# A tail search with fewer steps, and second experts' codes written to memory

## The chip, the cores and the metric

The kernel runs on one core of a Trainium2 chip. The metric is the device time of one execution in microseconds (us). The core's engines work side by side, each on its own queue in order: TensorE (PE, matrix products into PSUM), VectorE (DVE), ScalarE (ACT), GpSimd (POOL) and SyncE (SP, which issues most transfers). GpSimd issues the indirect transfers, those that gather or scatter rows by a list of indices.

## The reference

```python
attn = np.maximum(z @ z.T / S, 0) ** 2           # 4 batches, S = 3072, d_qk = 64
x = (u * (attn @ v)).reshape(12288, 256)
# first mixture: 8 experts of 1536 tokens each, tokens taken in falling order of logits
for idx in np.argsort(-(x @ w_gate).flatten()):
    tok, e = divmod(idx, 8)
    if assigned[tok] >= 0 or counts[e] >= 1536: continue
    assigned[tok] = e; counts[e] += 1
y[assigned == e] = relu(x[assigned == e] @ w1[e]) @ w2[e]
# second mixture: argmax expert, the first 384 tokens of each expert in order are kept
out[i] = gate[i] * (relu(y[i] @ w1b[e2]) @ w2b[e2]) if kept else 0
```

Since the second mixture keeps the first 384 tokens of each expert, the kernel runs the first mixture for the first 40 x 128 tokens alone and verifies at the end (`check`) that these were enough; a raised flag runs `general` over all tokens.

## The kernel before

There are four stages. **Attention** fills TensorE for the first 1106 us; each fp32 product is made of three with operands split into a high and a low part. Most of the routing is done beside it: a threshold splits the tokens into a head, whose experts are settled, and a tail, whose rows are scattered to a table `tt`.

**First mixture** (`ffn1`). Sixteen units in an order written out by hand: units 0 to 7 take 432 head tokens of each expert (4 tiles of at most 128 rows, table `TA`), units 8 to 15 take 256 tokens of each expert (2 tiles, table `TB`), which head and tail tokens fill up. A unit has 8 steps f = 0 to 7, each with 6 products of layer 1 (`L1013`) and, two steps behind, 6 of layer 2 (`L1163`). ScalarE makes `hH` and VectorE `hL` of each layer 1 result; weights are split by ScalarE (`pH`) and VectorE (`pL`, `L225`), four pieces a unit. Around the products hooks do the rest: rows of unit n+2 are gathered at f = 6 (`fetch`, on GpSimd), the next unit's rows are turned by TensorE, and the finished unit's rows with the second gate's logits (`yr`) are scattered to `ya` (`post`). `code` then finds each row's second expert: `first_hot` gives a number `M` per row. `hot` and `rh` (VectorE, one pair a tile) are one-hot rows of the token's place, and `mapping` multiplies them on TensorE into `pe2` (`L1150`), a table of 128 x 40 second experts that `table2` reads when the last unit is done. `slow` is a list of such VectorE work, taken one by one at fixed places (`trickle`).

**The tail search** (`tail`) runs beside units 0 to 7. It assigns 23 columns of tail tokens in 9 phases. In a phase, each token's best open expert `V`, `TH` is found; the threshold at which some expert runs full is found by three rounds of a grid of 32 values: VectorE compares (`gG`, `L856` for the first round and `L858` for the others), TensorE counts with 23 products (`L866`), the count is compared with the room left (`gO`, `L868`), a product spreads it (`L871`) and `gX` sums it. Then `NW` marks the chosen tokens, a product counts them (`L890`), and full experts are closed. After the phases a closing part gives each token a slot, builds the table `tabB` by 23 one-hot products (`L587`), and `tokens` turns it into index lists for units 8 to 15.

`tail` is a generator. Each `yield` names planner costs, and `Follow.step`, called after nearly every product of `ffn1`, issues the next step when it seems due: `tp` is TensorE's planned time (a product of w columns adds w/2400), `td` VectorE's. A step (pe, d, extra, lead) does this:

```python
m.tp += pe
m.dve(d, 0.2)                      # td = max(td, tp + 0.2) + d
self.ready = m.td + 0.15 - lead    # the next step waits until tp >= ready
m.td += extra
```

The fetch of unit 8 needs the lists, so in unit 7 at f = 3 `late` calls `p.finish()`, which issues all the steps that are left at once.

**Closing and second mixture.** `table2` ranks the second experts and builds lists by one-hot products; `ffn2` runs 8 units of 384 rows and scatters `orow` to the output.

Of the kernel before, what the change touches and what calls it, by code (L numbers as in the profile page):

```python
# [53 lines left out]
class Follow:  # L54
# [24 lines left out]
class Moe:  # L79
# [55 lines left out]
    def consts(self, wg1, wg2):  # L135
# [3 lines left out]
        self.idr = c.tile([128, 128], FR, name="idr")  # L139
        nc.scalar.activation(self.idr, self.idf, AF.Copy)  # L140
# [67 lines left out]
    def zero_tail(self):  # L208
        self.nc.sync.dma_start(self.tt.rearrange("(p c) k -> p (c k)", c=self.TC), self.zt[:, :self.TC * self.TW])
# [379 lines left out]
    def tokens(self, tj, tp, H, name, rows):  # L589
# [11 lines left out]
        nc.vector.scalar_tensor_tensor(s, f, -1.0, e, op0=OP.add, op1=OP.add)  # L601
        return dict(tj=tj, tp=tp, g=g, s=s)
# [78 lines left out]
    def prep(self):  # L681
# [71 lines left out]
        self.TA = self.tokens(self.tabH[:, 0], self.tabH[:, 1], 6 * E, "a", JF * 128)  # L753
# [30 lines left out]
    def tail(self, rows):  # L784
# [26 lines left out]
        nc.vector.tensor_scalar(iv, tok[:, :TD], 0.5, -1e36, op0=OP.is_lt, op1=OP.mult)  # L811
# [12 lines left out]
        nc.vector.scalar_tensor_tensor(LT[:, TD:], H[:, :, None].to_broadcast([128, 4, E]), -1e36,  # L824
# [3 lines left out]
        self.diag(k8, kcol)  # L828
        nc.vector.tensor_scalar(cl0, k8, 0.5, 0.0, op0=OP.is_lt, op1=OP.add, accum_out=cc)
        hi = self.t0  # L830
        PH = E + 1
        cl, c2, NW = cl0, cc, None
        for ph in range(PH):
            LM = R.tile(sh, F32, name="LM")
            nc.vector.scalar_tensor_tensor(LM, cl[:, None, :].to_broadcast(sh), -1e30, LT, op0=OP.mult, op1=OP.add)
            s3 = R.tile([128, 3], F32, name="s3")
            if ph:

                nc.vector.scalar_tensor_tensor(s3, sd[:, 0], d, sd[:, 1], op0=OP.mult, op1=OP.add)
                cc = c2  # L840
                yield 0.0, 0.5, 0.0, 0.5
            else:
                nc.vector.tensor_scalar(s3, w3, st, None, op0=OP.mult)
            V = R.tile([128, TC], F32, name="tV")
            nc.vector.tensor_reduce(V, LM, AX.X, OP.max)
            M = R.tile([128, NTH], F32, name="gM")
            nc.vector.tensor_scalar(M, self.mrow, s3[:, 0:1], hi, op0=OP.mult, op1=OP.add)
            TH = R.tile(sh, BF, name="tTH")
            nc.vector.tensor_tensor(TH, LM, V[:, :, None].to_broadcast(sh), OP.is_equal)
            yield 0.0, 0.85 if ph else 2.0, 0.0, 0.5  # L850
            for i in range(3):
                G = R.tile([128, TC, NTH], BF, name="gG", tag="gG", bufs=1)
                Vb = V[:, :, None].to_broadcast([128, TC, NTH])
                Mb = M[:, None, :].to_broadcast([128, TC, NTH])
                if i == 0:
                    nc.vector.tensor_tensor(G, Vb, Mb, OP.is_ge)  # L856
                else:
                    nc.vector.scalar_tensor_tensor(G, Vb, sn, Mb, op0=OP.subtract, op1=OP.is_ge)  # L858
                    hi = self.plus(hi, sn)
                if i < 2:  # L860
                    M = R.tile([128, NTH], F32, name="gM")
                    nc.vector.tensor_scalar(M, self.mrow, s3[:, i + 1:i + 2], hi, op0=OP.mult, op1=OP.add)
                yield 0.25, 1.2 if i else 0.9, 0.3
                pc = self.rt()
                for j in range(TC):
                    nc.tensor.matmul(pc[:E, :NTH], TH[:, j, :], G[:, j, :], start=j == 0, stop=j == TC - 1)  # L866
                over = R.tile([E, NTH], BF, name="gO")
                nc.vector.tensor_scalar(over, pc[:E, :NTH], kcol, None, op0=OP.is_gt)  # L868
                yield 0.6, 0.2
                pa = self.rt()  # L870
                nc.tensor.matmul(pa[:, :NTH], self.ones[:E, :], over, start=True, stop=True)  # L871
                x = R.tile([128, NTH], F32, name="gX")
                sn = R.tile([128, 1], F32, name="gn")
                nc.vector.scalar_tensor_tensor(x, pa[:, :NTH], 0.5, s3[:, i:i + 1].to_broadcast([128, NTH]),
                                               op0=OP.is_lt, op1=OP.mult, accum_out=sn)
            hi = self.plus(hi, sn)
            NW = R.tile(sh, BF, name="tNW")
            nc.vector.scalar_tensor_tensor(NW, V[:, :, None].to_broadcast(sh), hi, TH, op0=OP.is_ge, op1=OP.mult)
            nc.vector.scalar_tensor_tensor(LT, NW, 1e35, LT, op0=OP.mult, op1=OP.add)
            if ph < PH - 1:  # L880
                dd = R.tile([128, 3], F32, name="std")
                sd = R.tile([128, 2, 3], F32, name="stw")
                nc.vector.tensor_scalar(dd[:, 1:2], s3[:, 2:3], 1.0 / NTH, None, op0=OP.mult)
                nc.vector.tensor_scalar(dd[:, 0:1], hi, self.lo0, -1.0 / NTH, op0=OP.subtract, op1=OP.mult)
                nc.vector.tensor_scalar(sd[:, 1], w3, dd[:, 1:2], None, op0=OP.mult)
                nc.vector.tensor_tensor(dd[:, 2:3], dd[:, 0:1], dd[:, 1:2], OP.subtract)
                nc.vector.tensor_scalar(sd[:, 0], w3, dd[:, 2:3], None, op0=OP.mult)
            yield 0.25, 0.9, 1.0
            pn = self.rt()
            nc.tensor.matmul(pn[:, :TC * E], self.ones, NW.rearrange("p j g -> p (j g)"), start=True, stop=True)  # L890
            cn = R.tile([128, E], F32, name="tcn")
            nc.vector.tensor_reduce(cn, pn[:, :TC * E].rearrange("p (j g) -> p g j", g=E), AX.X, OP.add)
            if ph < PH - 1:
                cl = R.tile([128, E], F32, name="cl")
                c2 = R.tile([128, 1], F32, name="cc")
                d = R.tile([128, 1], F32, name="std2")
                nc.vector.scalar_tensor_tensor(cl, cn, 0.0, k8, op0=OP.add, op1=OP.is_ge, accum_out=c2)
                nc.vector.tensor_tensor(d, c2, cc, OP.is_gt)
                yield 0.3, 0.7, 0.0, 0.5
        self.over = c.tile([128, E], F32, name="ovr")  # L900
        nc.vector.tensor_tensor(self.over, cn, k8, OP.is_gt)
        yield 0.6
        FIN = R.tile(sh, BF, name="FIN", bufs=1)
        nc.vector.tensor_scalar(FIN, LT, 1e34, None, op0=OP.is_ge)

        NF = self.JF * 128
        m = R.tile([128, TC], F32, name="tm", bufs=1)
        nc.vector.tensor_scalar(m, tok, NF + 0.5, None, op0=OP.is_lt)
        oh = R.tile([128, E, TC], F32, name="toh", bufs=1)
        nc.vector.tensor_tensor(oh, FIN.rearrange("p j g -> p g j"), m[:, None, :].to_broadcast([128, E, TC]),  # L910
                                OP.mult)
        rs = c.tile([128, E, TC], F32, name="trs")
        nc.gpsimd.memset(rs, 1.0)
        nc.gpsimd.memset(rs[:, :, 0:1], 0.0)
        yield 0.6
        inc = R.tile([128, E, TC], F32, name="tinc", bufs=1)
        nc.vector.tensor_tensor_scan(inc.rearrange("p g j -> p (g j)"), rs.rearrange("p g j -> p (g j)"),
                                     oh.rearrange("p g j -> p (g j)"), 0.0, op0=OP.mult, op1=OP.add)
        tot = R.tile([128, E], BF, name="ttot", bufs=1)
        nc.vector.tensor_copy(tot, inc[:, :, TC - 1])  # L920
# [154 lines left out]
    def ffn1(self, units, W, keys, plan, src, dst, ncol, side0, G, X, late=()):  # L1075
# [100 lines left out]
        def hook(n, f):  # L1176
            if f == 3 and n > 1:
                mapping(n - 2)
# [328 lines left out]
def fast(ctx, tc, m, w1, w2, w1b, w2b, out, ahead, rows):  # L1507
    E = m.E
# [97 lines left out]
```

## Time and profile before

| what | value |
|---|---|
| median of three runs | 1636.5 us (1636.49 to 1637.97) |
| profiled execution | 1636.56 us |
| span of its instructions | 1634.8 us |
| TensorE busy | 1580.8 us (97%) |
| VectorE busy | 1186.5 us (73%) |
| ScalarE busy | 1116.7 us (68%) |
| GpSimd busy | 333.1 us (20%) |
| mean granted TensorE clock | 0.983 |

The profiled execution is 0.06 us from the median, so its views can stand for the runs. Products on TensorE are pipelined: a record's duration is longer than the distance to the next start, and the distance is the cost. A line number is that of the function that issues the instruction, so instructions of helpers are told apart by their tiles.

### The profile page before, as it was taken

How to read it: one execution, taken by the hardware profiler on the slowest of the kernel's cores; microseconds unless marked ns; L12 is line 12 of the kernel's file. 1: busy time of each engine (PE TensorE's matmuls, PEld its weight loads, DVE VectorE, ACT ScalarE, POOL GpSimd, SP SyncE). 2: the span in 40 equal slices, each digit the busy share in tenths (PEclk: the TensorE clock that was granted, in tenths of full speed). 3: DMA queues.
4: the chain of work that ended last, by engine and by line, in shares of the span. 5: the costliest groups of instructions: out<-in, count | busy, mean ns of one | idle time of the engine just before them, and what ended most of it. 6: DMA issues, size and time to landing. Idle time of an engine off the chain costs nothing.

```text
span 1634.8 us, 24914 instructions
## 1 busy us (share of the span) xinstructions
PE 1580.8 (97%) x8570; PEld 1326.7 (81%) x8570; DVE 1186.5 (73%) x2338; ACT 1116.7 (68%) x1937; POOL 333.1 (20%) x518
## 2 busy tenths in 40 slices
PE   8999999999999999999999999999999969989997
PEld 5888887888888888888887777878888759978997
DVE  6877788777778767777877877677777766775652
ACT  7877788777788877778987767884444316644552
POOL 1000000000000000000000478642333113323341
PEclk9999999999999999999999999999999969999999
DMA  6111355322335212224310112223343204644540
GB/s 136 20 27 33 68 136 133 73 70 76 72 67 130 76 46 59 59 66 86 77 33 21 28 20 45 60 80 118 101 124 103 84 19 134 189 134 124 153 129 28
DMA packets 282681, 132.44 MB, mean 81 GB/s; under 512 B 216717, under 2 KB 268173, under 8 KB 282544
## 3 DMA queue, kind: packets, MB, share of 16 engines
q1 hardware_dynamic: 269264, 106.90, 26.0%
q0 software_dynamic: 13280, 23.85, 5.0%
q8 instruction: 69, 1.13, 0.3%
q14 instruction: 68, 0.56, 0.1%
HBM read 84.61 MB, written 40.55 MB: 77 GB/s over the span
## 4 chain that ended last, share of the span: by engine, by line
PE 70%; issue 16%; DVE 7%; POOL 2%; ACT 2%; DMA 1%; SPq 1%; POOLq 0%; DVEq 0%
PE acc L397 12%; PE acc L398 12%; PE acc L399 12%; PE sc L1013 9%; PE sc L368 6%; PE sc L369 6%; PE acc L1163 5%; PE mi L1114 2%; DVE pL L225 1%; PE rt L866 1%; PE mi L336 1%; PE acc L1320 1%; PE acc L1321 1%; PE acc L1322 1%; DVE hL L1023 1%
## 5 line engine op out<-in xcount | busy, mean ns | idle before, releaser
L382 DVE TENSOR_TENSOR aL<-a,aH 128x512 fp32r<-128x512 f32 x576 | 398.6, 693 | 212.9 <-ACT a L377 157.8
L371 ACT ACTIVATE r<-sc 128x512 f32<-128x512 f32 x576 | 343.0, 595 | 186.6 <-PE sc L369 180.7
L397 PE MATMUL acc<-aH,pH 128*128 128x512 f32 x1152 | 449.7, 390 | 0.0
L398 PE MATMUL acc<-aL,pH 128*128 128x512 f32 x1152 | 449.0, 390 | 0.0
L399 PE MATMUL acc<-aH,pL 128*128 128x512 f32 x1152 | 448.5, 389 | 0.0
L379 DVE TENSOR_TENSOR a<-r 128x512 f32<-128x512 f32 x344 | 238.5, 693 | 43.0 <-ACT r L371 41.8
L397 PEld LDWEIGHTS acc<-aH,pH 128*128 128x128 f32 x1152 | 216.7, 188 | 45.6
L399 PEld LDWEIGHTS acc<-aH,pL 128*128 128x128 f32 x1152 | 216.7, 188 | 45.6
L398 PEld LDWEIGHTS acc<-aL,pH 128*128 128x128 f32 x1152 | 216.7, 188 | 45.5
L368 PE MATMUL sc<-zHL 128*128 128x512 f32 x576 | 229.8, 399 | 6.3 <-DVE zHL L280 6.0
L1021 ACT ACTIVATE hH<-sc 128x432 fp32r<-128x432 f32 (+2 forms) x192 | 90.0, 469 | 212.5 <-PE sc L1013 208.2
L369 PE MATMUL sc<-zLH,zHL 128*128 128x512 f32 x576 | 225.3, 391 | 0.2 <-DVE zLH L284 0.2
L380 ACT ACTIVATE aH<-r 128x512 fp32r<-128x512 f32 x344 | 217.8, 633 | 10.9
L347 POOL TENSOR_TENSOR lgs<-lgb 32x128 f32<-32x128 f32 x23 | 15.2, 659 | 853.2 <-DVE lgb L344 853.2
L376 ACT ACTIVATE aH<-r 128x512 fp32r<-128x512 f32 x232 | 146.7, 632 | 7.4
L1023 DVE SCALAR_TENSOR_TENSOR hL<-sc,hH 128x432 fp32r<-128x432 f32 (+2 forms) x192 | 99.3, 523 | 65.6 <-ACT hH L1021 65.4
L377 ACT ACTIVATE a<-r 128x512 f32<-128x512 f32 x232 | 142.8, 616 | 0.0
L368 PEld LDWEIGHTS sc<-zHL 128*128 128x128 f32 x576 | 108.7, 189 | 36.1 <-DVE zHL L280 7.4
L1013 PE MATMUL sc<-xTH,pH 128*128 128x384 f32 (+2 forms) x368 | 125.9, 342 | 5.9 <-DVE hL L1023 5.8
L369 PEld LDWEIGHTS sc<-zLH,zHL 128*128 128x128 f32 x576 | 108.8, 189 | 21.5 <-DVE zLH L284 0.5
L1013 PE MATMUL sc<-xTL,pH 128*128 128x384 f32 (+2 forms) x368 | 120.0, 326 | 0.0
L1013 PE MATMUL sc<-xTH,pL 128*128 128x384 f32 (+2 forms) x368 | 119.8, 326 | 0.0
(333 smaller groups left out, 2261.4 us busy)
## 6 DMA issues: line engine op xcount, KB each, us to landing
raw<-in_moe_w_dram SPq DMA_DIRECT2D x84, 512.0 KB, 3.7
raw<-in_v_dram SPq DMA_DIRECT2D x24, 512.0 KB, 4.3
uraw<-in_u_dram SPq DMA_DIRECT2D x192, 64.0 KB, 2.3
out_dram<-zt SPq DMA_DIRECT2D x24, 512.0 KB, 4.2
xb<-xT SPq DMA_DIRECT2D x14, 512.0 KB, 3.4
zr<-in_z_dram SPq DMA_DIRECT2D x96, 64.0 KB, 2.4
zLH<-zHL POOLq DMA_DIRECT2D x46, 128.0 KB, 2.3
ya<-zt SPq DMA_DIRECT2D x10, 544.0 KB, 3.5
```

The lines of the kernel that those rows point to most:

```text
L368: nc.tensor.matmul(p, lw, zHL[b, c % QC], start=True, stop=False)
L369: nc.tensor.matmul(p, lw, zLH[c], start=False, stop=True)
L371: nc.scalar.activation(r, p, AF.Relu, scale=SCALE)
L376: nc.scalar.activation(HS[s], r, AF.Square)
L377: nc.scalar.activation(a, r, AF.Square)
L379: nc.vector.tensor_tensor(a, r, r, OP.mult)
L380: nc.scalar.activation(HS[s], r, AF.Square)
L382: nc.vector.tensor_tensor(LS[s], a, HS[s].bitcast(F32), OP.subtract)
L397: nc.tensor.matmul(accs[h], vh[sl], HS[s], start=k == 0, stop=False)
L398: nc.tensor.matmul(accs[h], vh[sl], LS[s], start=False, stop=False)
L399: nc.tensor.matmul(accs[h], vl[sl], HS[s], start=False, stop=k == KT - 1)
L1013: nc.tensor.matmul(p, a, b[:, d, :w], start=i == 0, stop=i == 5)
```

## The change

**Search.** The grid is compared in units of the step: `U = (V - hi) / st`, so that the values compared with are constants (`m3`), and a position `N` takes the place of the moving upper end. The comparison with the room left goes from VectorE to ScalarE (a `Relu` with `-kcol` as bias), and so do `h`, `fine` and `dd`, once a phase. The yields become fewer and their numbers change; a new form of five numbers doesn't go through `td`. The constants 1e30 to 1e36 become multiples of the step (`mk`). Work that doesn't depend on the phases is moved ahead of them, the last count behind the table.

```diff
+                if len(y) == 5 if isinstance(y, tuple) else False:
+                    m.tp += y[0]
+                    self.ready = m.tp + y[4]
+                    return
...
-                yield 0.0, 0.5, 0.0, 0.5
...
-            yield 0.0, 0.85 if ph else 2.0, 0.0, 0.5
...
-                yield 0.25, 1.2 if i else 0.9, 0.3
...
-                nc.vector.tensor_scalar(over, pc[:E, :NTH], kcol, None, op0=OP.is_gt)
-                yield 0.6, 0.2
...
-            yield 0.25, 0.9, 1.0
...
-                nc.vector.tensor_tensor(d, c2, cc, OP.is_gt)
-                yield 0.3, 0.7, 0.0, 0.5
...
+            LM = R.tile(sh, F32, name="LM", bufs=1)
+            nc.vector.scalar_tensor_tensor(LM, cl[:, None, :].to_broadcast(sh), mk[:, 1:2], LT, op0=OP.mult, op1=OP.add)
+            V = R.tile([128, TC], F32, name="tV")
+            nc.vector.tensor_reduce(V, LM, AX.X, OP.max)
+            if ph:
+                d = R.tile([128, 1], F32, name="std2")
+                nc.vector.tensor_tensor(d, c2, cc, OP.is_gt)
+                st = R.tile([128, 1], F32, name="st")
+                nc.vector.scalar_tensor_tensor(st, dd, d, fine, op0=OP.mult, op1=OP.add)
+                cc = c2
+            U = R.tile([128, TC], F32, name="tU")
+            rs = R.tile([128, 1], F32, name="trs1")
+            nc.vector.reciprocal(rs, st)
+            nc.vector.tensor_scalar(U, V, hi, rs, op0=OP.subtract, op1=OP.mult)
+            for i in range(3):
...
+                if i == 0:
+                    nc.vector.tensor_tensor(G, bc(U), Mb, OP.is_le)
+                    TH = R.tile(sh, BF, name="tTH")
+                    nc.vector.tensor_tensor(TH, LM, V[:, :, None].to_broadcast(sh), OP.is_equal)
+                else:
+                    nc.vector.scalar_tensor_tensor(G, bc(U), N, Mb, op0=OP.subtract, op1=OP.is_le)
+                yield 0.25, 1.45 if i else 2.2
...
+                nc.scalar.activation(over, pc[:E, :NTH], AF.Relu, bias=kcol)
+                yield 0.8, 0.0, 0.0, 0.0, 0.45
...
+                N = self.plus(N, sn) if i else sn
...
+                nc.scalar.activation(h, N, AF.Identity, scale=st, bias=hi)
...
+                nc.scalar.activation(fine, st, AF.Copy, scale=float(NTH) ** -3)
...
+                nc.scalar.activation(dd, hi, AF.Abs, scale=1.0 / NTH, bias=lon)
+                nc.vector.scalar_tensor_tensor(dd, dd, -1.0, fine, op0=OP.mult, op1=OP.subtract)
+            nc.vector.scalar_tensor_tensor(LT, NW, mk[:, 0:1], LT, op0=OP.mult, op1=OP.add)
...
+            yield 0.25, 1.1, 0.5
```

**Closing part of the search.** The table covers only the slots that units 8 to 15 use, 2 columns per expert in place of 6, so its 23 products write 32 columns, not 96; the slots are computed in one code with fewer operations, and the yields ahead of the table go from five to two.

```diff
-        s = self.slot_code(inc, oh, TC)
-        yield 1.1
...
-        yield from self.table(px, s, TC, 6 * E, jv, pv, pool=False)
...
+        yield 0.25, 2.0
...
+        yield 0.3, 1.3
         px = self.rt("tabt")
+        yield from self.table(px, None, TC, 2 * E, jv, pv, pool=False, i=s)
```

**Codes through memory.** For units 0 to 12 (`ND` = 13) the number `M` of each row is scattered, one word a row, to a table `ea` in device memory, by index lists `c` that `tokens` makes; `hot`, `rh` and the products into `pe2` stay for the last three units. `ea` is zeroed in attention, read back in the last unit at f = 2 and added to `pe2`.

```diff
+            def put(t, h):
+                m = min(128, w - t * 128)
+                self.put_rows(ea, T["c"][:m, h:h + 1], M[0][:m, t:t + 1], ncol * 128 - 1, ecodes)
+
+            if n < ND:
+                self.slow.append((0.35, add))
+                self.slow.append((0.8, lambda: M.append(self.first_hot(lg, E, len(cols), None))))
+                self.slow.extend((0.0, lambda t=t, h=h: put(t, h)) for t, h in enumerate(cols))
+                return
...
+            if f == 2 and n == NU - 1:
+                self.pe2a = self.r1.tile([128, ncol], F32, name="pe2a%d" % ncol)
+                nc.sync.dma_start(self.pe2a, ea.rearrange("(p j) k -> p (j k)", p=128))
...
         mapping(NU - 1)
+        nc.vector.tensor_tensor(self.pe2a, self.pe2a, pe2[:, :ncol], OP.add)
```

**Buffers.** `idr`, which nothing reads, goes; the three `orow` tiles of a unit of `ffn2` become slices of one tile that shares `yT`'s buffer.

## Rows read from the trace of the kernel before

**Rows 1.** The page, part 2: 40 slices, busy tenths, granted clock in tenths.

```profile
PE   8999999999999999999999999999999969989997
...
PEclk9999999999999999999999999999999969999999
```

**Rows 2.** Windows: stretch, us, busy us by engine, PEclk, DMA share, GB/s.

```profile
1104.00:1303.40 199.40, 196.21 (x1447) 166.04 (x1445) 151.68 (x468) 83.59 (x145) 59.11 (x86) 1.00 0.35 108
1303.40:1331.80 28.40, 9.79 (x147) 7.33 (x147) 21.04 (x82) 0.00 (x0) 0.97 (x3) 0.54 0.02 6
1331.80:1338.00 6.20, 6.20 (x24) 5.71 (x22) 2.80 (x18) 0.93 (x2) 3.14 (x5) 0.62 0.14 42
1338.00:1458.50 120.50, 116.08 (x942) 112.87 (x940) 80.58 (x215) 71.34 (x147) 39.25 (x53) 1.00 0.51 154
```

**Rows 3.** Timeline of PE, 1301 to 1312.5: start us, us, instruction, idle before.

```profile
1301.27 0.37 PE L1150 MATMUL pe<-rh,hot 128*128 128x40 bf16 x4
1301.57 0.73 PE L1114 MATMUL mi<-sel,yT 128*128 128x136 f32 x4
...
1303.41 0.73 PE L866 MATMUL rt<-gG,tTH 128*8 128x32 bf16 x23
...
1308.16 0.31 PE L890 MATMUL rt<-tNW,ones 128*128 128x184 bf16 x1 [0.93 <-DVE tNW L878]
1311.80 0.78 PE L866 MATMUL rt<-gG,tTH 128*8 128x32 bf16 x23 [3.33 <-DVE gG L856]
```

**Rows 4.** Timeline of VectorE: the first grid of two search phases (six more between).

```profile
1122.42 0.92 DVE L856 TENSOR_TENSOR gG<-tV,gM 128x736 bf16<-128x736 f32 x1
...
1296.21 0.92 DVE L856 TENSOR_TENSOR gG<-tV,gM 128x736 bf16<-128x736 f32 x1
```

**Rows 5.** Groups of VectorE by form, 1104 to 1303: busy us, mean ns, idle.

```profile
L225 DVE TENSOR_TENSOR pL<-raw,pH 128x1024 fp32r<-128x1024 f32 x28 | 34.1, 1216 | 0.7 <-ACT pH L220 0.5
L858 DVE SCALAR_TENSOR_TENSOR gG<-tV,gn,gM 128x736 bf16<-128x736 f32 x15 | 14.8, 985 | 0.5
...
L1139 DVE TENSOR_SCALAR rh<-iob,tabH,fM 128x40 bf16<-128x40 bf16 x24 | 5.5, 291 | 0.0
L868 DVE TENSOR_SCALAR gO<-rt,kcol 8x32 bf16<-8x32 f32 x22 | 5.3, 239 | 21.7 <-PE rt L866 21.6
```

**Rows 6.** Waits of TensorE, 1104 to 1303: us in total, times, longest.

```profile
PE sc L1013 <- DVE hL L1023: 2.2, 4, 1.1
```

**Rows 7.** Groups of ScalarE by form, whole span.

```profile
L220 ACT ACTIVATE pH<-raw 128x1024 fp32r<-128x1024 f32 x80 | 84.1, 1051 | 0.0
...
L1021 ACT ACTIVATE hH<-sc 128x256 fp32r<-128x256 f32 x64 | 24.6, 384 | 35.1 <-PE sc L1013 34.2
...
L1345 ACT ACTIVATE orow<-acc,gt 128x256 f32<-128x256 f32 x16 | 7.6, 472 | 3.2 <-PE acc L1322 2.2
...
L1306 ACT ACTIVATE ex<-l 128x24 f32<-128x24 f32 x8 | 1.8, 223 | 8.7 <-DVE l L1304 8.6
L279 ACT ACT_TABLE_LOAD x1 | 1.3, 1283 | 0.7 <-PEq L1587 0.7
```

**Rows 8.** Timeline of GpSimd, 1180 to 1193.

```profile
1180.40 1.00 POOL L969 DMA_INDIRECT g<-xa,tkga  x1 [5.45 <-PE rt L871]
1181.70 0.97 POOL L969 DMA_INDIRECT g<-xa,tkga  x1 [0.30 <-issue]
...
1192.24 1.59 POOL L636 DMA_INDIRECT ya<-yr,tksa  x1 [6.11 <-ACT yr L1117]
```

**Rows 9.** Waits of TensorE, 1365 to 1458.

```profile
PE sc L1013 <- DVE hL L1023: 3.6, 6, 0.6
```

**Rows 10.** Timeline of VectorE, 1402 to 1403.

```profile
1402.50 0.49 DVE L1139 TENSOR_SCALAR rh<-iob,tabB,fM 128x40 bf16<-128x40 bf16 x2
1402.90 0.75 DVE L1023 SCALAR_TENSOR_TENSOR hL<-sc,hH 128x256 fp32r<-128x256 f32 x2
```

**Rows 11.** Timeline of VectorE, 1465.

```profile
1465.81 0.20 DVE L1254 TENSOR_TENSOR off<-s,off 128x40 f32<-128x40 f32 x1
```

More of the change, by code (lines that the diff above doesn't have):

```diff
@@ L587, in table, with tokens @@
                 nc.tensor.matmul(p[:, :2 * H], L[:, :, j], rf[:, :, j], start=o + j == 0, stop=o + j == ncol - 1)
-    def tokens(self, tj, tp, H, name, rows):
+    def tokens(self, tj, tp, H, name, rows, codes=False):
         nc = self.nc
@@ L601, in tokens @@
         nc.vector.scalar_tensor_tensor(s, f, -1.0, e, op0=OP.add, op1=OP.add)
+        if codes:
+            c = self.r1.tile([128, H], I32, name="tkc" + name)
+            nc.vector.scalar_tensor_tensor(q, tp, float(rows // 128), tj, op0=OP.mult, op1=OP.add)
+            nc.vector.scalar_tensor_tensor(c, q, -float(rows // 128), e, op0=OP.add, op1=OP.add)
+            return dict(tj=tj, tp=tp, g=g, s=s, c=c)
         return dict(tj=tj, tp=tp, g=g, s=s)
@@ L828, in tail @@
         self.diag(k8, kcol)
+        nc.vector.tensor_scalar(kcol, kcol, -1.0, None, op0=OP.mult)
         nc.vector.tensor_scalar(cl0, k8, 0.5, 0.0, op0=OP.is_lt, op1=OP.add, accum_out=cc)
[L830 to L840, printed above, removed]
-                yield 0.0, 0.5, 0.0, 0.5
[L842 to L849, printed above, removed]
-            yield 0.0, 0.85 if ph else 2.0, 0.0, 0.5
[L851 to L862, printed above, removed]
-                yield 0.25, 1.2 if i else 0.9, 0.3
[L864 to L867, printed above, removed]
-                nc.vector.tensor_scalar(over, pc[:E, :NTH], kcol, None, op0=OP.is_gt)
-                yield 0.6, 0.2
[L870 to L887, printed above, removed]
-            yield 0.25, 0.9, 1.0
[L889 to L897, printed above, removed]
-                nc.vector.tensor_tensor(d, c2, cc, OP.is_gt)
-                yield 0.3, 0.7, 0.0, 0.5
@@ L912, in tail @@
[L912 to L920, printed above, removed]
@@ new lines, in tail @@
+        early = R.tile([128, TC], F32, name="tm", bufs=1)
+        nc.vector.tensor_scalar(early, tok, NF + 0.5, None, op0=OP.is_lt)
+        rs1 = c.tile([128, E, TC], F32, name="trs")
+        nc.gpsimd.memset(rs1, 1.0)
+        nc.gpsimd.memset(rs1[:, :, 0:1], 0.0)
+        base = R.tile([128, E], F32, name="tbase", bufs=1)
+        nc.vector.tensor_scalar(base, self.hc, float(self.WA), 127.0 - self.WA, op0=OP.max, op1=OP.add)
+        nc.vector.scalar_tensor_tensor(base, self.iof[:, :E], 256.0, base, op0=OP.mult, op1=OP.add)
@@ L937, in tail @@
         nc.vector.tensor_scalar(pv, ti[:, 2], 1.0, None, op0=OP.add)
[L938 to L945 removed]
+        hi = self.t0
@@ new lines, in tail @@
+        oh = R.tile([128, E, TC], F32, name="toh", bufs=1)
+        nc.vector.scalar_tensor_tensor(oh, LT.rearrange("p j g -> p g j"), mk[:, 3:4],
+                                       early[:, None, :].to_broadcast([128, E, TC]), op0=OP.is_ge, op1=OP.mult)
+        inc = R.tile([128, E, TC], F32, name="tinc", bufs=1)
+        flat = lambda x: x.rearrange("p g j -> p (g j)")
+        nc.vector.tensor_tensor_scan(flat(inc), flat(rs1), flat(oh), 0.0, op0=OP.mult, op1=OP.add)
+        tot = R.tile([128, E], BF, name="ttot", bufs=1)
@@ new lines, in tail @@
+        nc.vector.tensor_copy(tot, inc[:, :, TC - 1])
+        yield 0.25, 2.0
+        p = self.rt()
+        nc.tensor.matmul(p[:, :E], self.low, tot, start=True, stop=True)
+        nc.vector.tensor_tensor(base, base, p[:, :E], OP.add)
+        nc.vector.tensor_tensor(inc, inc, base[:, :, None].to_broadcast([128, E, TC]), OP.add)
+        nc.vector.tensor_tensor(inc, inc, oh, OP.mult)
+        s = R.tile([128, TC], I32, name="scs%d" % TC, bufs=1)
+        with nc.allow_low_precision("whole numbers"):
+            nc.vector.tensor_reduce(s, inc.rearrange("p g j -> p j g"), AX.X, OP.add)
@@ new lines, in tail @@
+        yield 0.3, 1.3
+        px = self.rt("tabt")
+        yield from self.table(px, None, TC, 2 * E, jv, pv, pool=False, i=s)
+        tab = c.tile([128, 2, 2 * E], F32, name="tabB")
+        nc.vector.tensor_tensor(tab.rearrange("p a (e h) -> p a e h", h=2),
+                                px[:, :4 * E].rearrange("p (a e h) -> p a e h", a=2, h=2),
+                                self.tabH.rearrange("p a (e h) -> p a e h", h=6)[:, :, :, 4:6], OP.add)
+        self.TB.update(self.tokens(tab[:, 0], tab[:, 1], 2 * E, "b", NF, True))
@@ new lines, in tail @@
+        yield 0.7
+        FIN = R.tile(sh, BF, name="FIN", bufs=1)
+        nc.vector.tensor_scalar(FIN, LT, mk[:, 3:4], None, op0=OP.is_ge)
+        pn = self.rt()
+        nc.tensor.matmul(pn[:, :TC * E], self.ones, NW.rearrange("p j g -> p (j g)"), start=True, stop=True)
+        cn = R.tile([128, E], F32, name="tcn")
+        nc.vector.tensor_reduce(cn, pn[:, :TC * E].rearrange("p (j g) -> p g j", g=E), AX.X, OP.add)
+        self.over = c.tile([128, E], F32, name="ovr")
+        nc.vector.tensor_tensor(self.over, cn, k8, OP.is_gt)
@@ L1072, in pipeline, with ffn1 @@
             side(True)
-    def ffn1(self, units, W, keys, plan, src, dst, ncol, side0, G, X, late=()):
+    def ffn1(self, units, W, keys, plan, src, dst, ea, ncol, side0, G, X, late=()):
         nc, E, NF = self.nc, self.E, self.F // 128
-        pe2 = self.pe2 = self.px("pe2")
+        pe2 = self.px("pe2")
         NU = len(units)
-        last = sum((w + 127) // 128 for _, _, w, _ in units) - 1
+        ND = NU - 3
+        last = sum((w + 127) // 128 for _, _, w, _ in units[ND:]) - 1
+        ecodes = []
         scat, Y, ACC, YR, LG, HOT = [], {}, {}, {}, {}, {}
@@ L1339, in row @@
         def row(n, t):
-            o = self.f.tile([128, 256], F32, name="orow", bufs=3)
+            if t == 0:
+                O[n] = self.f.tile([128, 2, self.WA], F32, name="orow", tag="yT", bufs=1).rearrange("p a b -> p (a b)")
+            o = O[n][:, t * 256:(t + 1) * 256]
             g = GT[n][:, t:t + 1]
@@ L1499, in plan @@
             return {n: (y, m.wsrc(a, b, y), m.w) for n, (x, y) in enumerate(zip(keys, keys[1:])) if x != y}
-        m.ffn1(units, first(w1, w2), order, plan(order, w1, w2), xd, yd, NT, lambda: None, {}, {})
+        eg = m.dram.tile([m.N, 1], F32, name="eg")
+        nc.sync.dma_start(eg.rearrange("(p j) k -> p (j k)", p=128), m.zt[:, :NT])
+        m.ffn1(units, first(w1, w2), order, plan(order, w1, w2), xd, yd, eg, NT, lambda: None, {}, {})
         m.table2(NT)
@@ L1514, in fast @@
         seq = [(e, [6 * e + t for t in range(4)], m.WA, m.TA) for e in range(E)]
-        seq += [(e, [6 * e + 4 + t for t in range(2)], m.WB, m.TB) for e in back]
+        seq += [(e, [2 * e + t for t in range(2)], m.WB, m.TB) for e in back]
         keys = [u[0] + 2 * E * (n >= E + 3) for n, u in enumerate(seq)]
@@ L1526, in fast @@
         W = {0: ahead}
-        m.ffn1(seq, W, keys, plan, m.xa, m.ya, m.JF, p.step, {0: m.G0}, {0: m.X0}, {E: p.finish})
+        m.ffn1(seq, W, keys, plan, m.xa, m.ya, m.ea, m.JF, p.step, {0: m.G0}, {0: m.X0}, {E: p.finish})
         e2, s2 = m.table2(m.JF)
```

94 lines of the change are left out of this document (59 added, 35 removed).

## The prediction

> **What bounds the kernel now.** I read the strip of 40 slices first. TensorE is busy in nine tenths of nearly every slice, at full granted clock [rows 1]: what saves no TensorE time and ends no wait of TensorE saves nothing here. The strip has one early dent, in both its rows, at the slice that begins at 1308 us [rows 1]. The windows give its edges. From 1104 to 1303.4 TensorE has work for 196.21 of 199.40 us. From 1303.4 to 1331.8, 28.4 us, it is busy for 9.79 us, at 0.54 of its clock, while VectorE is busy for 21.04 and ScalarE for nothing. The next 6.2 us run at 0.62 of the clock; from then to 1458.5 TensorE is busy for 116.08 of 120.50 us [rows 2].
>
> The timeline says what the dent is. At 1303.41 the 23 little products of a count (L866) start, and from there on only instructions of the tail search follow on TensorE: it waits 0.93 us for `tNW`, then 3.33 us for the next phase's grid [rows 3]. That is `p.finish()`: the fetch of unit 8, in unit 7 at f = 3, needs the closing table, so every step of the search that is left is issued in one piece. Five of the 27 counts, the counting of the chosen and the table are left.
>
> Why is so much left? A phase of the search takes 24.8 us (1122.42 to 1296.21 is seven phases [rows 4]), nine phases take 223 us, and the deadline comes 181 us after the first grid. `Follow` sets the pace: each step adds its two numbers to `tp` and `td`, and the next one is issued when `tp` has passed `ready`. I added up these constants unit by unit (a matmul w/2400, a flush 0.5, a low part 1.2, the deferred list). The sums of the kernel before put a phase 21.7 planner us apart and leave off, at the deadline, just ahead of the second count of the eighth phase: five counts, as the trace has it. So the walk can be trusted for the order of the program.
>
> **The change, part by part.** The profiled execution took 1636.56 us with a span of 1634.8; the median is 1636.5, so differences from one hold for the other.
>
> *Search.* A phase has 7 steps in place of 10, and the three evictions to `gO` no longer go through `td`. The same walk with the new constants puts phases 14.4 planner us apart; in real time 24.8 x 14.4 / 21.7 = 16.5 us. The last step falls in unit 6 at f = 1, some 25 planner us ahead of the deadline. Nothing is left for `finish`, so the 28.4 us go. Their TensorE work stays, inside the stream: five counts at 0.73 plus a small product of 0.2, 4.6 us; the counting of the chosen and the prefix, 0.7; the table, 23 narrow products at the 0.075 us of the second expert's products (four start at 1301.27, the next instruction at 1301.57 [rows 3]), 1.7. Together 7.0, so the gain is **21.4 us**; if these products cost twice as much it is 14.4, and if they all hid in TensorE's idle it would be 28.4.
>
> *Clock.* The 6.2 us at 0.62, a mix of the two levels of 1.2 and 2.4 GHz, lose 6.2 x 0.38 = 2.4 us [rows 2]. Without 28 idle us ahead of them this goes too: **2.4 us**, between 0 and 2.4.
>
> *Codes through memory.* Of 48 products into `pe2`, 42 go: 42 x 0.075 = **3.2 us** of a busy TensorE. The 42 `hot` and 42 `rh` leave VectorE (an `rh` is 0.291 us [rows 5]). From 1365 to 1458 TensorE waits six times for `hL`, 3.6 us in all, at most 0.6 [rows 9], and one of these stands in the timeline of VectorE: two `rh` of 0.49 at 1402.50 hold the `hL` back to 1402.90 [rows 10]. Five of the six waits belong to units that lose their `rh`, and each is shorter by about those 0.40: **2.0 us**, between 0 and 3.0.
>
> In their place GpSimd issues 42 scatters of one word a row. Its nearest rows are gathers 1.30 us apart (1180.40, 1181.70). Four scatters are 5.2 us, behind the unit's four gathers, where GpSimd is idle for 6.11 us [rows 8]; the `yr` scatters queued behind them are read only after the last unit. So this costs nothing; with that cover gone it would be a delay of those `yr` scatters, for which nothing waits. The read of `ea` is one more transfer on SP, a unit and a half after the last scatter and most of a unit ahead of its use: nothing. Price if it were late: its landing, a few us at the closing.
>
> *Closing.* One addition of 40 columns stands between the last product and `table2`; a 0.20 us row of that shape [rows 11] plus a hand-over gives **0.25 us** lost. A zeroing transfer, two operations more in `tokens`, `idr` removed, and the shared `yT`/`orow` buffer lie beside TensorE's work, in attention or between uses a unit apart: nothing.
>
> *New waits of TensorE.* This is the open term. (a) A phase's first grid now depends on `d`, `st`, a reciprocal and `U` in a row. In the forced stretch the way from the product of the chosen (1308.16) to the first count (1311.80) took 3.6 us [rows 3] with five housekeeping operations in it that the new code spreads elsewhere; I take 3.4. The new constants leave 0.25 + 0.2 + 2.2 + 0.15 = 2.8 planner us, 3.2 real ones by the ratio above. Short by 0.2, and by some 0.3 where an `hL` or a `pL` (1.216 us [rows 5]) stands in front: 0.5 x 8 = 4 us. (b) `gO` moves to ScalarE, which is busy 83.59 of 199.40 us [rows 2], with `pH` of 1.051 us in its queue. There the eviction costs between 0.223 us (`ex`, 24 columns) and 0.31 (that plus the 0.088 by which `orow`, whose scale is a tile, exceeds `hH` of the same size [rows 7]), against 0.239 on VectorE [rows 5]. What waits behind it on ScalarE are `hH` of later products, so nothing that TensorE needs sooner; on VectorE it frees a queue that stood 21.7 us behind it [rows 5]. (c) Then ScalarE makes `h`, `fine` and `dd`; VectorE's `dd` waits for them with `LT` and any `hL` behind, about 0.5 us a phase, inside the 0.7 us that the step's constants leave. Bounds for a to c: nothing, or 8 x 1.22 for a `pL` in front of every phase and 27 x 0.42 x 0.53 for half a `pH` in front of every eviction, 15.8 us. The nearest row is that steps paced by the same bookkeeping cost TensorE 2.2 us from 1104 to 1303 [rows 6], so I stay near the low end: **4 us** lost.
>
> The Trainium skill ("ScalarE: Activation LUTs", Rules for kernel authors) sends relu to VectorE and not to ScalarE. By that rule the move of `gO` alone loses 27 x 0.07 = 1.9 us where TensorE waits for it, and the sum would be 2 us higher; the rows bear out the price (0.31 against 0.239) but also show VectorE's queue standing idle behind that very instruction, so I don't add it.
>
> Sum: -21.4 - 2.4 - 3.2 - 2.0 + 0.25 + 4 = -24.8, so **1611.7 us**.
>
> **Rivals.** *TensorE waits at most steps* (chance 0.12). The search runs one and a half times as dense, on engines whose queues hold `pL` and `pH`. At 0.45 us for each of 36 steps that is 16 us in place of 4: 1624; at 0.7 it is 1633. Against it: the walk gives a later count 2.05 planner us for a grid of 0.985 us [rows 5] and some 0.6 around it.
>
> *The search still runs into the deadline* (0.03). For it: nothing but the constants. Each phase left costs some 10 us, an estimate from the 28.4 us that held one and two thirds of a phase and the closing [rows 2]; with one left and half the clock loss, about 1623.
>
> *Table loads* (slower than before, 0.02). `Identity` and `Abs` are in no row; `Copy`, `Relu`, `Square` and `Exp` share one load of 1.283 us [rows 7]. If the two new functions needed other tables, each phase would pay four loads between the `Relu` of the stream: 8 x 4 x 1.28 = 41 us on ScalarE, in front of `hH`. If TensorE waits for all of it: 1653; from 25 us of it on the kernel is slower. The Trainium skill ("ScalarE: Activation LUTs", Table sets) has cheap functions, identity and abs among them, in every set; by it this costs nothing, and no run so far shows it.
>
> *The scatters show* (0.05). If GpSimd's records run long (one `yr` scatter took 1.59 [rows 8]), gathers come later; but the next gather is a unit away. If half of the 42 cost TensorE 0.3: 1618.
>
> **How the numbers follow.** The forecast has 0.78. Its own range, from the bounds of its terms, is 1604 (dearest hidden work free, no new waits) to 1620 (8 us more of them). The rest reaches to 1633 and beyond; 1604 to 1624 leaves out the worse half of the first rival, the table loads, and the rare mishap, under 2 in 10. About 0.2%, 3.3 us, is what a measurement tells from no change. Only the table loads, or a wait of 0.8 us at each of the 36 steps (29 us), end at or above 1633: faster 0.96, same 0.02, slower 0.02.
>
> **What would show it.** Right: no stretch over 2 us between 1290 and 1340 without TensorE, clock at 1.00 there; first grids some 16 us apart; the last of the tail before unit 7; six products into `pe`; one table load. Wrong: waits of TensorE for `gG` or `gO` above 6 us in all between 1104 and 1303, or the flag of `check` being raised, which would run `general` after all this.

## The result and the profile after

In four runs the changed kernel took 1620.0 us (median; 1618.49 to 1621.26), the kernel before on the same chip 1637.24: a ratio of 0.989, interval 0.988 to 0.991. The forecast was 1611.7, range 1604 to 1624: the sign and the range held, the point was 8.3 us too low. The profiled execution took 1618.49 us (before: 1636.56). The traces are cut here at the first and the last product of the first experts' stage (`ffn1`) and the last product of all:

| from ... to | before | after |
|---|---|---|
| start to first product of `ffn1` | 1106.2 | 1105.9 |
| `ffn1` | 352.0 | 330.7 |
| closing and `ffn2`, to the last product | 164.4 | 164.6 |
| last product to the end | 12.2 | 15.3 |

The forecast had 25.0 us gained in `ffn1`; it gained 21.3. It had nothing for the last row, which lost 3.1. The dent of [rows 1, 2] is gone. Windows of the kernel after, columns as in [rows 2]:

```profile
1105.90:1310.00 204.10, 195.30 (x1520) 161.88 (x1519) 154.59 (x446) 92.31 (x189) 83.81 (x131) 0.98 0.34 103
1310.00:1436.60 126.60, 125.19 (x983) 122.71 (x981) 77.14 (x183) 75.34 (x156) 66.22 (x97) 1.00 0.51 151
...
1120.00:1130.00 10.00, 8.70 (x75) 6.62 (x73) 8.19 (x19) 3.62 (x7) 2.48 (x2) 0.83 0.24 67
1220.00:1230.00 10.00, 7.74 (x54) 5.94 (x53) 7.68 (x19) 3.11 (x6) 8.12 (x13) 0.85 0.43 128
1300.00:1320.00 20.00, 20.00 (x110) 18.74 (x109) 7.60 (x19) 7.79 (x15) 8.81 (x16) 1.00 0.25 79
```

Where the forced stretch was, TensorE is busy all the time. After 1310 us it idles for 1.4 us, against 4.4 from 1338 on before [rows 2]. But in the search it idles for 8.8 us (before, ahead of the dent: 3.2 of 199.4 [rows 2]), and twice the granted clock falls from 2.4 to 1.2 GHz for a part of ten microseconds, to a mean of 0.83 and 0.85 over them: 3.2 us more. The waits of TensorE from 1104 to 1440, the answer to [rows 6, 9]:

```profile
PE sc L1045 <- DVE hL L1055: 5.1, 4, 2.3
PE rt L905 <- DVE tTH L899: 3.1, 4, 1.3
PE mi L1016 <- DVE xTL L1020: 1.1, 1, 1.1
PE acc L1207 <- DVE hL L1055: 0.8, 1, 0.8
```

The longest in the timeline of VectorE, and under it that of TensorE:

```profile
1220.48 1.22 DVE L231 TENSOR_TENSOR pL<-raw,pH 128x1024 fp32r<-128x1024 f32 x1
1221.61 0.34 DVE L934 TENSOR_REDUCE tcn<-rt 128x8 f32<-128x184 f32 x1
...
1222.20 0.41 DVE L877 SCALAR_TENSOR_TENSOR LM<-cl,mk,LT 128x184 f32<-128x184 f32 x1
...
1223.87 0.93 DVE L897 TENSOR_TENSOR gG<-tU,mrow 128x736 bf16<-128x736 f32 x1
1224.72 0.34 DVE L899 TENSOR_TENSOR tTH<-LM,tV 128x184 bf16<-128x184 f32 x1
1224.98 1.11 DVE L1055 SCALAR_TENSOR_TENSOR hL<-sc,hH 128x432 fp32r<-128x432 f32 x2
...
1225.63 0.46 PE L1045 MATMUL sc<-xTH,pH 128*128 128x432 f32 x1 [2.27 <-DVE hL L1055]
```

One step of the search starts a phase: from `tcn` at 1221.61 to `tTH` at 1224.98 VectorE works on nothing else, 3.4 us, and two `hL` that TensorE needs stand behind it. The forecast had an `hL` in front of the grid; it is the other way round.

The end, on GpSimd's sequencer, before and then after (duration ns min/median/max, first and last start):

```profile
L1570 POOLq INC_SWDGE_SEM  x1: 1115/1115/1115, 1628.6 to 1628.6; - x1
L1601 POOLq DRAIN  x3: 46/107/3831, 1629.7 to 1634.1; - x3
...
L1622 POOLq INC_SWDGE_SEM  x1: 1875/1875/1875, 1606.8 to 1606.8; - x1
L1653 POOLq DRAIN  x3: 46/107/6934, 1608.7 to 1616.2; - x3
```

Before, the first and the longest of the second took 1.12 and 3.83 us; now 1.88 and 6.93. Together 8.81 for 4.95: 3.86 us more, of which the last row of the table shows 3.1.

### The profile page after: what moved, and what is told of

It reads as the page before. It is cut to its first block, busy times and chain, and to the rows that moved or that the text cites. A ratio compares the mean times of both kernels' runs of the same rounds, so it can differ in the third digit from the quotient of the medians.

```text
span 1616.5 us, 24872 instructions
## 1 busy us (share of the span) xinstructions
PE 1574.3 (97%) x8526; PEld 1320.5 (82%) x8528; DVE 1163.1 (72%) x2187; ACT 1128.8 (70%) x1987; POOL 382.6 (24%) x602
## 4 chain that ended last, share of the span: by engine, by line
PE 74%; issue 16%; DVE 4%; POOL 1%; ACT 1%; DMA 1%; SPq 1%; POOLq 0%; DVEq 0%
PE acc L403 12%; PE acc L404 12%; PE acc L405 12%; PE sc L1045 10%; PE acc L1207 7%; PE sc L374 6%; PE sc L375 6%; PE mi L1149 1%; PE rt L905 1%; PE mi L342 1%; PE acc L1368 1%; PE acc L1369 1%; PE acc L1370 1%; PE mi L1016 1%; SPq L413 1%
```

## The experiments

All times are medians of four to six runs (twelve for one), beside the kernel before on the same chip: 1637.8 us for the first four kernels (`x_products`, `x_vector`, `x_split`, `x_twice`), 1637.0 for the next four (`x_pace`, `x_zero`, `x_pad32`, `x_pad42rows`).

**Search alone, and VectorE's eviction.** `x_products` sets `ND = 0`:

```
-        ND = NU - 3
+        ND = 0
```

> The new search and the new closing, but the codes of all second experts made by one-hot products again, as in the kernel before: no scatter into ea. Theory: the codes through memory are worth 42 products x 0.075 = 3.2 us of TensorE and some 2 to 3 us of waits for hL from 1310 us on, and they cost 3.1 us at the end of the program, because GpSimd's last drain (6.93 us after, 3.83 us before) grows with the number of DMAs that GpSimd itself has issued. So here the last product ends 5 to 6 us later against the changed kernel and the stretch behind it shrinks from 15.3 to 12.2 us: 1620.0 + 2 to 3 = 1622 to 1623 us. Rival: the longer drain has nothing to do with the scatters. Then the end stays at 15.3 us and the time is 1625 to 1626 us.

Measured: 1626.1 us, ratio 0.993 (0.992 to 0.994). `ffn1` takes 341.7 us, 11.0 more than after (5 to 6 expected; the forecast had 5.2); the end is back at 12.3, with the 1.12 and 3.83 us of before in its last two instructions. So the codes through memory are worth 11.0 us by the traces and give back 3.0. These traces are of the slowest of five executions here and the fastest of four after; the medians differ by 6.1 us, so by them the codes are worth some 9. TensorE idles 5.9 us more than after and is busy for 5.2 more, and its longest waits are for VectorE:

```profile
PE sc L1045 <- DVE hL L1055: 8.5, 11, 1.6
PE rt L905 <- DVE tTH L899: 3.4, 4, 1.3
PE sc L1045 <- DVE xTL L1020: 2.0, 1, 2.0
```

`x_vector` puts `gO` back on VectorE:

```
-                nc.scalar.activation(over, pc[:E, :NTH], AF.Relu, bias=kcol)
+                nc.vector.tensor_scalar(over, pc[:E, :NTH], kcol, 0.0, op0=OP.add, op1=OP.is_gt)
```

> The changed kernel with the 27 evictions of the counts to gO on VectorE again (one tensor_scalar), pacing numbers untouched. Theory: on ScalarE the eviction costs TensorE little (0.27 us each against 0.24, behind work that is seldom long), while on VectorE every one of the 27 holds whatever is queued behind it until its product has ended: 1 to 3 us slower, 1621 to 1623 us, with more of TensorE's waits put down to hL. Rival (relu on ScalarE is the dear choice): 1.9 us faster, 1618 us.

Measured: 1626.7 us, ratio 0.994 (0.992 to 0.995). `ffn1` takes 337.4 us, 6.7 more. `gO` is now a thing that TensorE waits for:

```profile
PE sc L1045 <- DVE hL L1055: 5.0, 4, 2.3
PE rt L910 <- DVE gO L907: 3.3, 4, 2.0
PE rt L905 <- DVE tTH L899: 3.2, 4, 1.3
```

Half of the 6.7 us is idle time (13.6 for 10.2), half a longer busy time (323.8 for 320.5), at a clock of 0.97 for 0.98 from the first product to 1310. The pacing still counts `gO` as off VectorE, so some of it may be pace.

**The start of a phase.** `x_split` cuts that step in two:

```
             nc.vector.tensor_reduce(V, LM, AX.X, OP.max)
             if ph:
+                yield 0.25, 1.2
...
-                yield 0.25, 1.45 if i else 2.2
+                yield 0.25 if i or not ph else 0.0, 1.45 if i else 1.8 if ph else 2.2
```

> The changed kernel with the start of a phase cut into two steps, between the largest logit (tV) and the new step width (st), so that a pending hL can be issued between them; the pacing numbers are 1.6 and 1.8 in place of 2.2. Theory: the waits of TensorE from 1104 to 1440 us that I mis-sized come from the 3.4 us of VectorE work at the start of a phase with hL queued behind it, and the clock falls after the two longest of them. Then the waits for hL fall from 5.1 us to below 2.5, those for tTH from 3.1 to below 1.5, the stretch of 1220 to 1250 us stays at full clock, and the time is 5 us lower: 1615 us. Rival (TensorE waits because ScalarE holds the eviction to gO behind pH and hH): the waits stay, 1619 to 1621 us.

(The numbers of the kernel that ran are 1.2 and 1.8.) Measured: 1612.8 us, ratio 0.985 (0.984 to 0.986). `ffn1` takes 322.3 us, 8.4 less than after. The step numbers go up too, so a phase is also paced later. Waits for `hL` fell from 5.9 to 3.4 in all, and in this execution the clock is 1.00 throughout `ffn1`. Windows:

```profile
1106.40:1310.00 203.60, 199.91 (x1564) 169.50 (x1563) 155.12 (x449) 95.95 (x196) 86.55 (x134) 1.00 0.35 105
...
1120.00:1130.00 10.00, 8.70 (x82) 6.63 (x81) 9.07 (x27) 3.63 (x7) 2.66 (x3) 1.00 0.21 69
```

And the waits of TensorE:

```profile
PE sc L1046 <- DVE hL L1056: 2.6, 4, 0.7
PE rt L906 <- DVE tTH L900: 1.3, 1, 1.3
```

Is it the cut, or only that a phase has more time? `x_pace` leaves the step whole and writes 3.2 for 2.2:

> The changed kernel with the start of a phase left in one piece, but paced later: 3.2 in place of 2.2, so that a phase takes about as many planner microseconds as in the kernel with the cut. It tells the cut from the slower pace. Theory (the cut matters, since hL waits behind 3.4 us of VectorE work however late the next step comes): waits for tTH fall to 1.5 us or less, those for hL stay at 4 us or more, and the time is 1617 us. Rival (only the pace was too tight): waits for hL fall below 2.6 us too, 1613 us as with the cut.

Measured: 1616.9 us, ratio 0.987 (0.986 to 0.989), `ffn1` 328.4. As the theory had it:

```profile
PE sc L1045 <- DVE hL L1055: 4.2, 5, 1.1
PE mi L1016 <- DVE xTL L1020: 1.6, 2, 0.8
PE rt L905 <- DVE tTH L899: 1.3, 1, 1.3
```

Pace alone takes most of the waits for `tTH` and one of the two falls of the clock; most of those for `hL` need the cut. Of the 8.4 us of the traces 2.2 are then pace and 6.2 the cut, but 1.7 of the 6.2 are a fall of the clock that the cut doesn't explain. The same stall from 1120 to 1130 lowers it in `x_pace` and not in `x_split`:

```profile
1120.00:1130.00 10.00, 8.70 (x76) 6.63 (x74) 8.72 (x26) 3.29 (x6) 1.82 (x2) 0.83 0.20 65
```

By the medians 7.2 us were gained, 3.1 by pace and 4.1 by the cut. So the cut is worth 4 to 4.5 us and the pace 2 to 3.

**What the 11.0 us of the codes are.** `x_zero` adds 42 products of zeros where the products of the codes stood:

```
+            if f == 3 and 0 <= n - 2 < ND:
+                zero(n - 2)
```

> The changed kernel with 42 products of a tile of zeros added where the products of the codes stood, of their shape and into the same accumulator; nothing is added on VectorE, and the codes still go through memory. It parts the 11.0 us by which the products shortened the first experts' stage when they went into TensorE's own time and VectorE's. Theory: the products themselves cost 42 x 0.075 = 3.2 us and the rest was VectorE work (hot and rh) that held hL back: the stage grows from 330.7 to 334 us and the time is 1623 us. Rival: a narrow product between the wide ones costs TensorE far more than 0.075 us: the stage grows by 8 us or more, 1628 us.

Measured: 1623.9 us (1619.9 to 1624.1), ratio 0.992 (0.990 to 0.993). In the profiled execution, the fastest of the five, `ffn1` is 1.7 us longer; the medians differ by some 3.6. The two agree when the clock is counted: that execution has one fall of it, worth 1.7 us, where the one of the kernel after has two.

```profile
1120.00:1130.00 10.00, 8.68 (x81) 6.62 (x79) 8.93 (x18) 3.38 (x7) 4.02 (x4) 1.00 0.39 105
1220.00:1230.00 10.00, 7.73 (x53) 6.24 (x52) 6.29 (x15) 3.54 (x8) 5.89 (x11) 0.83 0.39 123
```

So the products cost about 3.5 us, the smaller part, and the rival's 8 us is refuted. The other part was to be measured by `x_hot`, which makes `hot` and `rh` and uses them for nothing:

```
             if n < ND:
+                self.slow.extend((0.2, lambda h=h: hot_p(h)) for h in cols)
                 self.slow.append((0.35, add))
                 self.slow.append((0.8, lambda: M.append(self.first_hot(lg, E, len(cols), None))))
+                self.slow.extend((0.25, lambda t=t, h=h: hot_j(t, h)) for t, h in enumerate(cols))
```

> The changed kernel, codes through memory as in it, with the 42 hot and 42 rh of the first thirteen units made on VectorE too and used by nothing. With the run of the 42 products of zeros (first experts' stage 1.7 us longer) it splits the 11.0 us by which that stage is longer when the codes are made by products. Theory: VectorE's part is the rest, 9 us: the stage grows from 330.7 to 338 to 340 us, the waits for hL come back (6 to 9 us in all from 1104 us to the end of the stage), and the time is 1628 us. Rival: neither part alone costs much, since TensorE's waits come where both meet: under 4 us, 1624 us or less.

Measured: 1664.6 us, on a chip where the kernel before takes 1660.8; ratio 1.002 (1.000 to 1.004). This decides nothing: there everything is longer, attention too (first product of `ffn1` at 1126.8), and the kernel after wasn't run there. See the last section.

**The end of the program.** `x_twice` issues every scatter of a code a second time, into a buffer of its own:

```
                 self.put_rows(ea, T["c"][:m, h:h + 1], M[0][:m, t:t + 1], ncol * 128 - 1, ecodes)
+                if ncol == self.JF:
+                    self.put_rows(self.eb, T["c"][:m, h:h + 1], M[0][:m, t:t + 1], ncol * 128 - 1, twice)
```

> The changed kernel with each of the 42 scatters of codes issued a second time, into a buffer that nothing reads. Theory (the last drain grows with the number of GpSimd's own DMAs, 3.1 us for 42): the stretch from the last product to the end grows from 15.3 to 18.4 us and the time to 1623 us, while the stretch of the first experts' products keeps its length within 1 us. Rival (the drain is long for another reason): 15.3 us, 1620 us. Second rival (scatters delay what is queued behind them on GpSimd): the first experts' products end more than 2 us later.

Measured: 1618.1 us, ratio 0.988 (0.987 to 0.990). The theory of a growing drain failed as stated: the end shrank to 8.8 us.

```profile
L1625 POOLq INC_SWDGE_SEM  x1: 480/480/480, 1612.1 to 1612.1; - x1
L1656 POOLq DRAIN  x3: 46/107/1217, 1612.6 to 1614.4; - x3
```

`ffn1` is 3.7 us longer, nearly all one wait:

```profile
PE mi L1150 <- ACT yr L1153: 3.3, 1, 3.3
```

Eight code scatters of unit 7 stand ahead of the next unit's `yr` scatters, and ScalarE waits for one of these before it writes the next `yr`. That is the second rival. So the number of DMAs plays a part, but not on one slope, and three more numbers were tried. `x_pad32` is the kernel with the cut and 32 more scatters of 128 rows, `x_pad42rows` the same with 42 of 16 rows, `x_pad24` the changed kernel with 24 of 128:

> The kernel with the cut at the start of a phase (1612.8 us), and 32 scatters of codes of the first eight units issued a second time into a buffer that nothing reads, so 356 DMAs on GpSimd in place of 324. Theory: GpSimd's last two instructions are a sawtooth over the number of its DMAs, rising 0.092 us with each (4.95 us with 282 of them, 8.81 with 324) and falling back once on the way to 366 (1.70). If 356 lies behind the fall, the stretch from the last product to the end is 8 us in place of 15.9 and the time 1605 us; if ahead of it, 19 us and 1616 us. Rival (the number has no part in it): 15.9 us, 1613 us.

> The kernel with the cut at the start of a phase (1612.8 us), and 42 more scatters as in the run that issued each scatter twice, but with 16 rows each in place of up to 128. It tells the number of DMAs from the number of rows. Theory by number: the stretch from the last product to the end is 8.8 us as with 42 full scatters, and the time 1606 us. Theory by rows: 42 x 16 = 672 rows are a seventh of the 4,736 that added 3.9 us, so the stretch is 16.5 us and the time 1613 us.

> The changed kernel with 24 scatters of 128 rows more, of the codes of the first six units, into a buffer that nothing reads: 348 DMAs on GpSimd. Theory: as with 32 more, GpSimd's last two instructions fall to about 1 us from 8.8, the stretch from the last product to the end to 8 to 9 us from 15.2, and no yr waits, because the last of these scatters stands before the second experts' units: 1620.0 - 7 = 1613 us. Rival: the fall comes only behind 348 DMAs; then the two instructions take 11 us and the time is 1622 us.

| kernel | DMAs of GpSimd | INC_SWDGE_SEM + DRAIN, us | us, ratio |
|---|---|---|---|
| before, `x_products` | 282 | 4.95 | |
| after, `x_split` | 324 | 8.81 | |
| `x_pad24` | 348 | 11.45 | 1687.1, 1.014 (1.010 to 1.018) |
| `x_pad42rows` | 366, 42 of 16 rows | 12.88 | 1620.0, 0.989 (0.987 to 0.991) |
| `x_pad32` | 356 | 1.29 | 1610.2, 0.983 (0.982 to 0.985) |
| `x_twice` | 366 | 1.70 | 1618.1 |

The two instructions rise by 0.09 to 0.11 us with each DMA, whatever its rows: 42 of 16 rows added 4.07 us, the 42 of the change 3.86. Somewhere between 348 and 356 they fall back, but with short scatters not by 366. So both theories of `x_pad42rows` were wrong (19.9 us from the last product to the end, not 8.8 or 16.5), and what makes them fall is open. By the rows of the added scatters the kernels do stand in one order: with 672 (`x_pad42rows`) and 3072 (`x_pad24`) there is no fall, with 4096 (`x_pad32`) and 4736 (`x_twice`) there is. That would fit a rise with each DMA and a fall by rows; no run tests it. `x_pad32` is the fastest kernel measured: its end is 9.2 us, though its `ffn1` is 5.4 longer than with the cut alone, 3.0 of it the same wait for `yr`. The time of `x_pad24` is from the chip of `x_hot`, where the kernel before takes 1660.8 us. The chip doesn't show in the two instructions: with 324 DMAs `x_hot` has the 1.88 and 6.93 us of the others.

**A version with all of it.** `x_best` has the cut, 24 scatters of padding, and `yield 0.25, 2.0` ahead of the first phase. It was run twice:

> The cut at the start of a phase (1612.8 us), a second cut ahead of the first phase's largest logit, and the 24 scatters of padding. Theory: the cut ahead of the first phase takes away the 1.3 us wait for tTH (about 1 to 2 us), the padding 7 us at the end: 1604 us, with the search still ended before unit 7. Rival: the slower pace of the phases leaves steps for the deadline of the closing, which would show as a dent near 1310 us and cost 10 us or more: 1615 us.

> The cut at the start of a phase, a second cut ahead of the first phase's largest logit, and the 24 scatters of padding, a second time, because in the first run every kernel of the call, the kernel before too, ran 20 us and more longer than elsewhere, with stops of ScalarE and VectorE of up to 7 us. Theory: those stops came with that chip; 1604 us with the kernel before at 1637, the stretch from the last product to the end 8 to 9 us. Rival: the stops belong to this kernel's order of instructions; then they are there again and the time is above 1620 us.

Measured: 1687.7 us, ratio 1.016 (1.012 to 1.019), and 1685.2, ratio 1.014 (1.011 to 1.018), on two different chips, where the kernel before takes 1660.8 and 1660.7. The theory failed twice over. The padding misses the fall and costs 2.6 us at the end. The rest is not one dent: from 1160 to 1360 TensorE idles 6.5 to 8.6 us in every 40. Windows of the first of the two:

```profile
1160.00:1200.00 40.00, 31.45 (x255) 24.96 (x252) 21.30 (x60) 13.98 (x32) 17.83 (x29) 0.91 0.26 79
...
1240.00:1280.00 40.00, 31.80 (x231) 25.75 (x231) 23.19 (x66) 15.11 (x33) 18.00 (x30) 0.91 0.26 76
```

The theory of `x_best2`, that the stops came with the first of the two chips, failed: on the second they stand at the same places. One of the longest of ScalarE ends 64.3 us behind the first product of `ffn1` in the first run and 64.2 in the second:

```profile
1184.27 0.53 ACT L1056 ACTIVATE hH<-sc 128x432 fp32r<-128x432 f32 x1 [7.18 <-remote]
1193.86 0.53 ACT L1056 ACTIVATE hH<-sc 128x432 fp32r<-128x432 f32 x1 [7.09 <-remote]
```

So where they stand goes with the kernel's order, as the rival had it; `x_split`, on another chip, leaves ScalarE idle for no more than 3 us at a time in its first eight units. That the chips have a part too shows in the kernel before, 24 us longer on both. And the search is late again: `tabB` is made at 1369.3 in the first run, behind the first product of unit 7's f = 3 at 1365.9, the deadline (after: 1287.5). Whether this order would pay on the first chips wasn't tried.

## Why the prediction was right in sign and range, and short by 8 us

- *Forced stretch and clock* (21.4 and 2.4 predicted): right, the stretch is gone. No instruction of the tail is left for the deadline; the test of `ovr`, among the last, runs at 1291.3 in unit 6, and the stretch after 1300 is full at clock 1.00. The phases are 17.2 us apart (nine first grids from 1121.6 to 1259.1), 16.5 predicted.
- *Codes* (5.2): half the size. With the new search around them, making the codes by products costs 11.0 us by the traces, some 9 by the medians. The products themselves are about 3.5 us of it (3.2 predicted). 5.9 are idle time of TensorE (2.0 predicted), with longer waits for `hL` and `xTL`; the rest is open. That VectorE's 42 `hot` and 42 `rh` are what holds these back is argued from the releasers, not shown.
- *New waits of TensorE* (4 us): the term that failed, and the one I had called open. Idle outside the forced stretch was 7.6 us before and is 10.2 after, and the clock loses 3.2. Together that is 6 us lost where the sum had 4 lost and 2.0 gained. With the codes made by products it is more: in `x_products` TensorE idles 16.1 us and the clock loses 3.4, together 12 us more than the 7.6 before. Two things were missing. I priced the start of a phase by what TensorE waits for the grid, not by the `hL` queued behind 3.4 us of VectorE work; and I counted waits without the fall of the clock behind them, although [rows 2] showed one. `x_split`, later pace and cut together, gets 8.4 us back by its trace, 7.2 by its median.
- *Luck in the sum*: `x_products` has the search and the closing without the codes, and its `ffn1` is 10.3 us shorter than before; the terms for this (21.4, 2.4 and the 4 lost) make 19.8. The codes, taken after it, bring 11.0 for 5.2. One part is 9.5 us short and the other 5.8 over, where the whole of `ffn1` is 3.7 off.
- *`gO` on ScalarE*: 0.263 to 0.280 us, inside the bounds of 0.223 and 0.31, and worth more than thought. The rule of the Trainium skill ("ScalarE: Activation LUTs", Rules for kernel authors) would have the move lose 1.9 us; undoing it cost 6.7. The rule is about the price per element; in `x_vector` TensorE waits 3.3 us for `gO` in VectorE's queue, and the clock falls further. How much of the 6.7 is pace isn't told apart.
- *Table loads*: one load, of 1.283 us, as before. The Trainium skill's statement on table sets ("ScalarE: Activation LUTs", Table sets) agrees.
- *Scatters cost nothing*: wrong. They are hidden in the stream, as said (most are 1.0 us on GpSimd and 1.3 apart), but 42 more DMAs lengthen GpSimd's last two instructions by 3.86 us, and the end by 3.1. No row of before was read there: the sum took the last 12 us of the program as fixed. Nor is it so that nothing waits for a late `yr` scatter: in `x_twice` TensorE waits 3.3 us.
- *Closing* (0.25): 0.24. The addition of 40 columns takes 0.20 us, 0.27 behind the last product.

3.7 us from `ffn1` and 3.1 from the end make 6.8 of the 8.3; the other 1.5 are the median over the profiled execution, the fastest of four.

## What to carry to other kernels

Where steps of a side job are slipped into an in-order stream, look not only at what the step waits for, but at how long it holds its engine and what the main work has queued behind it: cutting one step in two and pacing it later brought 7 us more, 4 of them by the cut, where the whole change had brought 17. Add to the price of a wait of a microsecond or more the fall of the clock that may come with it. Work that leaves the critical path through GpSimd's own DMAs isn't free at the end of the program: read the last lines of each sequencer too.

## What was not expected of the hardware

- GpSimd's INC_SWDGE_SEM and DRAIN at the end: 4.95, 8.81, 11.45, then 1.29 us for 282, 324, 348, 356 DMAs of its own, and with 366 either 1.70 or, where 42 of them have 16 rows, 12.88. The kernels with the same DMAs agree to 0.01 us.
- A stall doesn't always lower the clock. From 1120 to 1130 TensorE is busy for 8.70 of 10 us in the kernel after, `x_pace` and `x_split`, at 0.83, 0.83 and 1.00. So single traces of two kernels can differ by a fall, 1.7 us, that neither made.
- On two chips (`x_hot`, `x_pad24` and the first `x_best` on one, the second `x_best` on the other) the kernel before takes 1660.8 and 1660.7 us, and hand-overs between engines come late. `gO` starts up to 5.07 us after its count's last product in `x_best`, at most 0.57 in `x_split`. The timeline of ScalarE in the first `x_best`, where the count had ended at 1219.4:

```profile
1220.68 0.40 ACT L1155 ACTIVATE yr<-mi 128x272 f32<-128x272 f32 x1
1224.49 0.28 ACT L910 ACTIVATE gO<-rt,kcol 8x32 bf16<-8x32 f32 x1 [3.41 <-remote]
```

What holds it back is not in the trace. The kernels differ there too: `x_hot`, without padding, takes 1664.6 us and `x_pad24` 1687.1 on the same chip, of which the end explains 2.6. `ffn1` is 17.6 longer with the padding (368.2 for 350.6); on the other chips `x_twice`, with more scatters, is 3.7 longer than after. Why isn't shown. The changed kernel and `x_split` weren't run there, so whether they win on such a chip stays open.
